# A transpose of 128 rows in place of one of 64, in a routed expert layer on one core

## The chip, the cores and the metric

The kernel runs on one core of a Trainium2 chip. The metric is device time in microseconds of one execution; times are medians of several runs. The core has five engines that run their own instruction streams in order and meet through semaphores: TensorE (PE, matmuls and transposes; its weight loads are shown apart as PEld), VectorE (DVE), ScalarE (ACT), GpSimd (POOL) and SyncE (SP, which issues most DMAs).

## What is computed

Three layers one after the other, on 2 x 576 = 1152 tokens of 512 numbers: an attention with 8 heads that keeps the 32 largest scores of a row; a dense layer with `h * cos(h)`; and a layer of eight experts, to which each token goes by its largest logit. Only the last is touched by the change:

```python
for i in range(N):
    e = expert_idx[i]
    if counts[e] < capacity:          # capacity 288
        disp[e, counts[e]] = x[i]
        pos[i] = counts[e]; counts[e] += 1; keep[i] = True
h = np.maximum(np.einsum('ecd,edf->ecf', disp, w1), 0.0)   # 512 -> 1024
y = np.einsum('ecf,efd->ecd', h, w2)                       # 1024 -> 512
for i in range(N):
    if keep[i]:
        out[i] = gate_w[i] * y[expert_idx[i], pos[i]]
```

All is in float32. Matrix products of full precision are made of two parts (`hi` rounded, `lo` the rest), as three products of a faster type.

## The kernel before

Each token's row is scattered to a DRAM buffer `xs` with `CAP` = 288 slots of `RW` = 520 numbers for each expert: 512 data, then the gate, then the token's number. The expert part works on the first `MAIN` = 192 slots of each expert; if any expert had more tokens, a conditional part (`more`, from L1055) would take the other 96, and it did not run here.

For each of the eight experts `e`:

- `gather(e)`, L949: SP brings the slots to SBUF. Slots 0 to 127 go to part 0 of `xg`, with a slot on each partition (L953). Slots 128 to 191 go to part 1, twice: to partitions 0 to 63 with all columns, and to partitions 64 to 127 with the columns from 512 on only, gate and token (L956, the loop over `a`). DVE casts the token numbers to `ti` (L958). Then come four chunks `c` of 128 columns: PE transposes part 0 (128 rows, L963) and part 1 (64 rows, L964) to a PSUM buffer `xp`, a ring of two buffers; ACT rounds the 192 columns to `xgs` (L966) and DVE subtracts to get the low part (L967). This frees the buffer.
- `expert_in(e, fc)`, L970: eight blocks, each with 4 x 2 matmuls to `hp` (L978, L980), which ACT and DVE add, clamp and split to `hc` (L983 to L991).
- `expert_out(e, a)`, L996: two output blocks `yp`, 8 units of three matmuls for slots 0 to 127 and 8 units of two for the rest (L1009), scaled with the gate by ACT (L1024, L1027) and DVE (L1029) and scattered by POOL (L1015).
- `weights2(e, i)`, L931: the float32 weights, 8 transfers of 512 KB for each expert (L936, L939), are split by ACT (`wh`, L944) and DVE (`wl`, L946), one expert or more ahead. They are kept in two sets of buffers, one for even and one for odd experts.

The order of the instructions on each engine is worked out before the program is built, by class `Plan` (L49 to L209). Each operation is declared with an engine, a cost in us, what it reads and writes, and a rank. `emit` then walks a modelled time: for each engine it takes, among the operations that could start within 0.02 us of the earliest one (L163), the one of lowest rank. It models the latency from an engine to its users (L57, `LAT`: 0.2 from PE, 0.16 from ACT, 0.14 from DVE), rings that give a buffer back after its last reader, 0.09 us for PE at a change of the kind of its output (L185), and a half clock of PE after little work (L189). Two figures of a declaration are touched: the cost of a pair of transposes, 0.4, and the number that goes with it, `duty` 0.5. The ranks put the transposes of expert `e` just ahead of the `yp` blocks of expert `e - 1`:

```python
R("rank", 90.0 + 10 * e - prm["ga"])     # L1038, ga = 4.016
gather(e)
...
R("rank", 96.0 + 10 * e + 2 * a)         # L1044
expert_out(e, a)
```

In the modelled time a gather costs SP 1.0 and the DMA 1.6 (L957).

Of the kernel before, what the change touches and what calls it, by code (L numbers as in the profile page):

```python
# [19 lines left out]
T = B * S  # L20
DM = H * D
FF = 2048
NE, F2 = 8, 1024
CAP = 288
SLOTS = NE * CAP
RW = 520
# [10 lines left out]
MAIN = 192  # L37
# [214 lines left out]
def forward(ctx, lasting, tc, kq, vn, vs_, w_in, w_out, w_gate, w1, w2, out, paired):  # L252
    nc = tc.nc
    PE, ACT, DVE, POOL, SP = nc.tensor, nc.scalar, nc.vector, nc.gpsimd, nc.sync
    prm = PRM if paired else FULL
    P = Plan(prm["tb"])
    T = P.T
# [16 lines left out]
    xs = lasting("xs", None, None)  # L274


    ident = lasting("ident", [128, 128], F32)
# [671 lines left out]
    def gather(e):  # L949
        kx = ("xg", e)  # L950

        def ld():
            SP.dma_start(T[kx][:, 0, :], xs[e * CAP:e * CAP + 128, :])  # L953
            for a in range(2):
                c = a * DM
                SP.dma_start(T[kx][64 * a:64 * a + 64, 1, c:RW], xs[e * CAP + 128:e * CAP + MAIN, c:RW])  # L956
        P.dma(1.0, 1.6, ld, r=[("xs", t) for t in range(9)], w=[kx])  # L957
        P.op("dve", 0.1, lambda: DVE.tensor_copy(T["ti", e], T[kx][:, :, DM + 1]), r=[kx], w=[("ti", e)])  # L958
        for c in range(4):
            kp, ks = ("xp", (e, c)), ("xgs", (e, c))  # L960

            def tr(c=c, kp=kp):
                PE.transpose(T[kp][:, 0:128], T[kx][:, 0, c * 128:(c + 1) * 128], ident)  # L963
                PE.transpose(T[kp][:, 128:MAIN], T[kx][0:64, 1, c * 128:(c + 1) * 128], ident[0:64, 0:64])  # L964
            P.op("pe", 0.4, tr, r=[kx], w=[kp], duty=0.5)
            P.op("act", 0.25, lambda kp=kp, ks=ks: ACT.activation(T[ks][:, 0], T[kp][:, 0:MAIN], AF.Copy), r=[kp], w=[ks])  # L966
            P.op("dve", 0.27, lambda kp=kp, ks=ks: DVE.tensor_tensor(  # L967
                out=T[ks][:, 1], in0=T[kp][:, 0:MAIN], in1=T[ks][:, 0], op=OP.subtract), r=[kp], w=[ks])
# [65 lines left out]
    for e in range(NE):  # L1034
        for i in range(8):
            R("rank", 90.0 + 10 * (e - 1) + 5 + i)
            weights2(e, i)
        R("rank", 90.0 + 10 * e - prm["ga"])  # L1038
        gather(e)
        for fc in range(8):  # L1040
            R("rank", 91.0 + 10 * e + 0.5 * fc)
            expert_in(e, fc)
        for a in range(2):
            R("rank", 96.0 + 10 * e + 2 * a)  # L1044
            expert_out(e, a)
# [90 lines left out]
```

## Time and profile before

| | |
|---|---|
| median of the runs | 705.67 us (705.2 to 707.3) |
| the profiled execution, its own time | 706.96 us |
| its span, first to last instruction | 705.1 us |
| PE busy | 596.7 us (85%) |
| DVE busy | 553.4 us (78%) |
| ACT busy | 496.0 us (70%) |
| mean granted clock of TensorE | 0.951 of full |

The expert part begins with the first gather at 523.84 us and ends with the last scatter at 698.7 us. "Busy" of PE counts overlapping records once; the end of a matmul's record is modelled, so the distance from one start to the next tells what an instruction takes of PE. The weight load of a matmul is a record of its own on PEld. A line "[0.17 <-DVE xgs L967]" behind an instruction says that its engine was idle for 0.17 us before it, and what ended that.

### The profile page before, as it was taken

Reading aid. Unit: us, or ns where it says so; the run is one execution under the profiler, and the core shown is the slowest. Engines: PE = TensorE matmul, PEld = TensorE weight load, DVE = VectorE, ACT = ScalarE, POOL = GpSimd, SP = SyncE. Lnnn points to the kernel's source line nnn. Section 1 sums busy time; section 2 is a strip of 40 time slices with the busy share of each in tenths; the row PEclk is TensorE's granted clock in tenths of the full one; section 3 lists DMA queues with packets and bytes.
Section 4 is the critical chain, followed back from the end, with each engine's and each line's share of the span. In section 5 each row is a group of like instructions: output and inputs, shape, how many; then the busy total and the mean of one; then the engine's idle time right before and its main releaser. Section 6 shows DMA issues by size and latency. Waiting matters only on the chain.

```text
span 705.1 us, 11071 instructions
## 1 busy us (share of the span) xinstructions
PE 596.7 (85%) x3611; PEld 434.8 (62%) x3611; DVE 553.4 (78%) x1654; ACT 496.0 (70%) x1004; POOL 265.2 (38%) x316
## 2 busy tenths in 40 slices
PE   3333576898999999989999899999639999999994
PEld 1122355645776655866665676666328888888893
DVE  5999999999999899999999953566115777779630
ACT  4666998999799988778877764476015777777630
POOL 3366675677345544554544432223110110011111
PEclk9999868999899999999999999999857999999998
DMA  8543552064221201100000003444023777778200
GB/s 330 198 150 122 164 163 91 1 236 172 67 89 39 76 0 38 35 1 17 1 1 1 1 17 119 140 144 150 31 78 119 230 241 223 226 257 254 71 17 16
DMA packets 29635, 76.24 MB, mean 108 GB/s; under 512 B 3966, under 2 KB 3966, under 8 KB 29568
## 3 DMA queue, kind: packets, MB, share of 16 engines
q1 hardware_dynamic: 27824, 70.68, 30.3%
q0 software_dynamic: 1744, 4.76, 1.8%
q8 instruction: 30, 0.49, 0.3%
q14 instruction: 37, 0.30, 0.2%
HBM read 63.52 MB, written 12.69 MB: 108 GB/s over the span
## 4 chain that ended last, share of the span: by engine, by line
PE 41%; DVE 34%; ACT 16%; DMA 3%; issue 3%; POOL 1%; SPq 1%; POOLq 0%; DVEq 0%; ACTq 0%
PE yp L1009 11%; DVE W L513 9%; DVE C L517 8%; PE hp L978 7%; PE x L729 7%; DVE C L509 4%; PE hp L980 3%; ACT Sp L561 2%; ACT pen L556 2%; DVE W L522 2%; DVE wt L405 2%; ACT Sp L570 2%; ACT Sp L494 2%; PE h L684 2%; DVE Sp L574 2%
## 5 line engine op out<-in xcount | busy, mean ns | idle before, releaser
L729 PE MATMUL x<-wo,hs 128*128 128x512 f32 x288 | 138.2, 603 | 0.0
L946 DVE TENSOR_TENSOR wl<-raw,wh 128x512 fp32r<-128x512 f32 x128 | 90.4, 741 | 41.9 <-ACT wh L944 38.7
L559 POOL TENSOR_TENSOR Sp<-Sp,pen 128x576 f32<-128x576 f32 x72 | 97.5, 1354 | 64.8 <-ACT pen L556 64.5
L513 DVE MAX8 W<-C 128x8 f32<-128x288 f32 x288 | 118.2, 446 | 0.6
L517 DVE MATCH_REPLACE8 C<-W,C 128x288 f32<-128x288 f32 x216 | 93.8, 440 | 0.0
L589 PE MATMUL pt<-ident,Sp 128*128 128x128 f32 x324 | 56.4, 304 | 38.6 <-ACT Sp L570 31.6
L482 PE MATMUL S<-kq 64*128 64x288 f32 x256 | 58.4, 539 | 30.8 <-ACT Sp L494 20.9
L944 ACT ACTIVATE wh<-raw 128x512 fp32r<-128x512 f32 x128 | 74.5, 622 | 9.9 <-DMA raw<-in_w_dram 6.9
L589 PEld LDWEIGHTS pt<-ident,Sp 128*128 128x128 f32 x324 | 40.4, 154 | 66.1 <-ACT Sp L570 41.0
L684 PE MATMUL h<-xh,wh 128*128 128x256 f32 x256 | 78.0, 305 | 0.5 <-ACT hs L691 0.4
L1015 POOL DMA_INDIRECT out_dram<-ot,ti x16 | 17.9, 1117 | 159.0 <-ACT ot L1024 124.8
L978 PE MATMUL hp<-xgs,wh 128*128 128x384 f32 x256 | 76.9, 370 | 0.0
L729 PEld LDWEIGHTS x<-wo,hs 128*128 128x128 f32 x288 | 49.0, 190 | 43.4 <-issue 42.7
L685 PE MATMUL h<-xl,wh 128*128 128x256 f32 x256 | 71.9, 281 | 0.0
L686 PE MATMUL h<-xh,wl 128*128 128x256 f32 x256 | 71.8, 281 | 0.0
L1009 PE MATMUL yp<-wh,hc 128*128 128x512 f32 x192 | 70.1, 405 | 0.0
L509 DVE TENSOR_TENSOR C<-Sp 128x576 f32<-128x576 f32 x72 | 64.5, 896 | 3.7 <-ACT Sp L494 2.9
L720 POOL TENSOR_TENSOR hs<-hs,ur 128x512 f32<-128x512 f32 x36 | 48.4, 1353 | 46.5 <-ACT ur L712 45.1
L980 PE MATMUL hp<-xgs,wl 128*128 128x192 f32 x256 | 65.5, 256 | 0.0
L561 ACT ACTIVATE Sp<-Sp,tb 128x576 f32<-128x576 f32 x72 | 55.7, 774 | 13.1 <-POOL Sp L559 12.9
L556 ACT ACTIVATE pen<-Sp,tb 128x576 bf16<-128x576 f32 x72 | 55.3, 768 | 6.3 <-POOL tb L549 5.5
L591 ACT ACTIVATE PT<-pt 128x384 f32<-128x384 f32 x108 | 48.5, 483 | 12.1 <-PE pt L589 12.0
(138 smaller groups left out, 1371.8 us busy)
## 6 DMA issues: line engine op xcount, KB each, us to landing
raw<-in_w_dram SPq DMA_DIRECT2D x64, 512.0 KB, 3.9
wraw<-in_w_out_dram SPq DMA_DIRECT2D x16, 512.0 KB, 3.9
wraw<-in_w_in_dram SPq DMA_DIRECT2D x16, 512.0 KB, 3.9
xs<-z SPq DMA_DIRECT2D x1, 4680.0 KB, 16.0
kq<-in_kq_dram SPq DMA_DIRECT2D x8, 576.0 KB, 7.8
v<-in_vn_dram SPq DMA_DIRECT2D x8, 320.0 KB, 5.5
v<-in_vs_dram SPq DMA_DIRECT2D x8, 320.0 KB, 3.0
out_dram<-z SPq DMA_DIRECT2D x1, 2304.0 KB, 21.0
```

The source lines that it names most:

```text
L509: DVE.tensor_tensor(out=T["C", s], in0=x[:, :, 0:HS], in1=x[:, :, HS:S], op=op)
L513: P.op("dve", 0.365, lambda r=r, i=i: DVE.max(T["W", s][:, i, LIST[r]:LIST[r] + 8], T["C", s][:, i, :]), r=[("C", s, i)], w=[("W", s, i)])
L517: P.op("dve", 0.42, lambda r=r, i=i: DVE.match_replace(T["C", s][:, i, :], T["W", s][:, i, LIST[r]:LIST[r] + 8], T["C", s][:, i, :], NEG), ...
L559: P.op("pool", 1.34, lambda i=i, kp=kp: POOL.tensor_tensor(out=T["Sp", s][:, i, :], in0=T["Sp", s][:, i, :], in1=T[kp], op=OP.subtract), r ...
L589: PE.transpose(T[kp][:, c * 128:(c + 1) * 128], P2[:, cc * 128:(cc + 1) * 128], ident)
L684: PE.matmul(o, hi, a, start=(kc == 0), stop=False, skip_group_check=True)
L729: P.op("pe", 0.86, lambda f=f, a=a: PE.matmul(T["x2", t], T[kh][:, a:a + 128], T["wo", 0][:, f, :], start=(f == 0), stop=(f == 15)), r=[kh ...
L944: P.op("act", 0.52, lambda a=a, hi=hi: ACT.activation(T[hi], T[kr][:, a * 512:(a + 1) * 512], AF.Copy), r=[kr], w=[hi])
L946: P.op("dve", 0.6, lambda a=a, hi=hi, lo=lo: DVE.tensor_tensor(out=T[lo], in0=T[kr][:, a * 512:(a + 1) * 512], in1=T[hi], op=OP.subtract), ...
L978: PE.matmul(T[kp][:, 0:2 * MAIN], T[ka][:, c:c + 128], x.rearrange("p a n -> p (a n)"), start=(kc == 0), stop=False, skip_group_check=True)
L980: PE.matmul(T[kp][:, 0:MAIN], T[kb][:, c:c + 128], x[:, 0], start=False, stop=(kc == 3), skip_group_check=True)
L1009: PE.matmul(T[kp], x, w, start=(fc + n == 0), stop=(fc == 7 and n == len(uses) - 1))
```

## The change

In `gather`, part 1 of `xg` gets the data columns of slots 128 to 255, on all 128 partitions, in one transfer of 128 rows of 512 numbers. (For the last 64 of these slots nothing of the result is used.) Gate and token columns of slots 128 to 191 come in two transfers of 64 rows of 8 numbers, to both halves of the partitions. A gather is then four DMAs, where it was three. The second transpose of a chunk reads 128 rows and writes columns 128 to 255 of `xp`; ACT and DVE still read 192 columns. The declared cost of the pair of transposes is 0.25 where it was 0.4.

```diff
         def ld():
             SP.dma_start(T[kx][:, 0, :], xs[e * CAP:e * CAP + 128, :])
+
+            SP.dma_start(T[kx][:, 1, 0:DM], xs[e * CAP + 128:e * CAP + 256, 0:DM])
             for a in range(2):
-                c = a * DM
-                SP.dma_start(T[kx][64 * a:64 * a + 64, 1, c:RW], xs[e * CAP + 128:e * CAP + MAIN, c:RW])
+                SP.dma_start(T[kx][64 * a:64 * a + 64, 1, DM:RW], xs[e * CAP + 128:e * CAP + MAIN, DM:RW])
...
                 PE.transpose(T[kp][:, 0:128], T[kx][:, 0, c * 128:(c + 1) * 128], ident)
-                PE.transpose(T[kp][:, 128:MAIN], T[kx][0:64, 1, c * 128:(c + 1) * 128], ident[0:64, 0:64])
-            P.op("pe", 0.4, tr, r=[kx], w=[kp], duty=0.5)
+                PE.transpose(T[kp][:, 128:256], T[kx][:, 1, c * 128:(c + 1) * 128], ident)
+            P.op("pe", 0.25, tr, r=[kx], w=[kp], duty=0.5)
```

## Rows read from the trace of the kernel before

**Rows 1.** Stretches: length, busy PE, PEld, DVE, ACT, POOL, granted clock, DMA share, GB/s.
```profile
596.70:605.00 8.30, 8.30 (x60) 8.30 (x59) 8.15 (x25) 7.40 (x21) 1.38 (x1) 1.00 0.96 311
605.00:617.00 12.00, 12.00 (x56) 9.17 (x55) 8.15 (x23) 8.03 (x20) 0.97 (x1) 1.00 0.59 187
```
**Rows 2.** The chain that ended last, from 560 to 700 us, shares by line.
```profile
by line: PE yp L1009 48.7%; PE hp L978 29.2%; PE hp L980 13.2%; PE xp L964 3.5%; PE xp L963 2.7%; DVE ot L1029 0.5%; ACT ot L1027 0.5%; POOL out_dram L1015 0.5%; POOLq L1053 0.4%; issue 0.1%
```
**Rows 3.** All instructions of L964: count, duration in ns (min/median/max), starts, form.
```profile
L964 PE MATMUL xp<-ident,xg x32: 271/272/367, 527.5 to 668.6; 64*128 64x64 f32 x32
```
**Rows 4.** PE in order of time, 604.5 to 609.5: start us, us, instruction.
```profile
605.57 0.27 PE L963 MATMUL xp<-ident,xg 128*128 128x128 f32 x1
605.77 0.27 PE L964 MATMUL xp<-ident,xg 64*128 64x64 f32 x1
...
606.44 0.50 PE L1009 MATMUL yp<-wh,hc 128*128 128x512 f32 x1
606.78 0.39 PE L1009 MATMUL yp<-wl,hc 128*128 128x512 f32 x1
607.01 0.40 PE L1009 MATMUL yp<-wh,hc 128*128 128x512 f32 x1
607.25 0.27 PE L963 MATMUL xp<-ident,xg 128*128 128x128 f32 x1
...
607.65 0.51 PE L1009 MATMUL yp<-wh,hc 128*128 128x512 f32 x1
608.00 0.40 PE L1009 MATMUL yp<-wl,hc 128*128 128x512 f32 x1
...
608.47 0.27 PE L963 MATMUL xp<-ident,xg 128*128 128x128 f32 x1
...
608.87 0.50 PE L1009 MATMUL yp<-wh,hc 128*128 128x512 f32 x1
```
**Rows 5.** PE in order of time, 318.3 to 319.5, attention part.
```profile
318.36 0.28 PE L686 MATMUL h<-xh,wl 128*128 128x256 f32 x1
318.47 0.82 PE L589 MATMUL pt<-ident,Sp 128*128 128x128 f32 x6
319.05 0.36 PE L684 MATMUL h<-xh,wh 128*128 128x256 f32 x1
319.25 0.28 PE L685 MATMUL h<-xl,wh 128*128 128x256 f32 x1
```
**Rows 6.** DVE in order of time, 604 to 611.
```profile
606.73 0.35 DVE L967 TENSOR_TENSOR xgs<-xp,xgs 128x192 fp32r<-128x192 f32 x1
...
607.93 0.35 DVE L967 TENSOR_TENSOR xgs<-xp,xgs 128x192 fp32r<-128x192 f32 x1
```
**Rows 7.** Weight loads in order of time, 604.5 to 609.5.
```profile
607.13 0.14 PEld L963 LDWEIGHTS xp<-ident,xg 128*128 128x128 f32 x1 [0.17 <-DVE xgs L967]
```
**Rows 8.** All engines in order of time, 517 to 534: the first two gathers.
```profile
526.04 1.09 SPq L956 DMA_DIRECT2D xg<-xs  x2
...
530.38 0.17 DVE L958 CAST ti<-xg 128x2 int32<-128x2 f32 x1 [1.64 <-DMA xg<-xs]
530.45 0.62 DVE L967 TENSOR_TENSOR xgs<-xp,xgs 128x192 fp32r<-128x192 f32 x2
...
531.56 0.69 PE L978 MATMUL hp<-xgs,wh 128*128 128x384 f32 x1
```
**Rows 9.** Stretches on both sides of the clock's rise, columns as in rows 1.
```profile
534.05:537.46 3.41, 3.41 (x14) 3.41 (x14) 1.27 (x5) 1.39 (x4) 0.00 (x0) 0.50 0.02 5
537.46:540.90 3.44, 3.44 (x26) 3.44 (x25) 2.68 (x9) 2.91 (x8) 0.00 (x0) 1.00 0.00 0
```
**Rows 10.** DMA issues by line: count, size of one, median us from issue to landing.
```profile
xg<-xs SPq DMA_DIRECT2D x8, 260.0 KB, 4.9
xg<-xs SPq DMA_DIRECT2D x8, 130.0 KB, 5.2
```
**Rows 11.** SP's DMA issues in order of time, 530 to 706: an expert's second and third.
```profile
598.78 1.10 SPq L956 DMA_DIRECT2D xg<-xs  x2
```

## The prediction

> **What bounds the kernel now.** I read the page for the span, then the busy time by stretch, then the chain of waits, then TensorE instruction by instruction. In the expert part TensorE (PE) is the bound: in the 8.30 us of an `hp` stretch and in the 12.00 us of the `yp` stretch behind it, it is busy for all of 8.30 and 12.00 us, while the vector engine (DVE) has 8.15 of each [rows 1]. The chain that ended last runs there almost only over PE, and 3.5 and 2.7 per cent of its 140 us, 8.7 us, stand on the two transposes, L964 and L963 [rows 2]. So PE time taken out of a transpose comes off the end, one for one, unless another engine is late next. DVE in the `hp` stretch (8.15 of 8.30 us) is the candidate.
>
> **The transposes.** There are 32 of the 64-row kind [rows 3], four in each of eight experts, each paired with one of 128 rows. I count by starts, since the records overlap. In the expert whose transposes begin at 605.57, L963 is followed after 0.20 us by L964, and the two first pairs end where the next `yp` matmul starts, at 606.44: 0.87 us [rows 4]. That matmul is followed by the next after 0.34 us, where 0.23 is usual (606.78 to 607.01): 0.11 more, which belongs to leaving the transposes. The third pair takes 0.40 us (607.25 to 607.65) and then 0.35 before the next one, 0.12 too many; the fourth takes 0.40 (608.47 to 608.87), and I give it the same 0.11 [rows 4]. Sum: 0.87 + 0.11 + 0.40 + 0.12 + 0.40 + 0.11 = 2.01 us for eight transposes, 0.25 each.
>
> Transposes of 128x128 alone stand in the attention part, at the same granted clock. Six in a row start at 318.47; the matmul behind them starts at 319.05 and its follower at 319.25; a matmul of that size otherwise takes 0.11 (318.36 to 318.47) [rows 5]. So six cost 319.25 - 318.47 - 0.11 = 0.67 us with their exit, 0.11 each. What differs in L964 is the tile: 64 rows and 64 columns of the array. After the change all eight of an expert are of the cheap kind: 8 x 0.11 = 0.88, which saves 1.13 us for an expert if nothing else is late.
>
> [...]
>
> **Does DVE let PE have it?** The buffer ring `xp` has two entries. The third pair needs the first entry back, which DVE frees with L967. Already now it begins with 0.17 us of waiting for it [rows 7]. L967 of the first chunk starts at 606.73 and takes 0.35; that of the second starts at 607.93 [rows 6], so the releases come at 607.08 and 608.28. DVE is full before that, so I hold these two times fixed. With cheap pairs and the order of instructions kept (two pairs, one unit of three `yp` matmuls at 0.70, a pair, a unit, a pair), PE would want the third pair at 605.57 + 0.44 + 0.70 = 606.71, and would wait to about 607.17; the fourth at 607.17 + 0.22 + 0.70 = 608.09, and would wait to 608.37, where it starts at 608.47 now. Then only 0.10 + (0.51 - 0.22) = 0.39 us of the 1.13 is left.
>
> But the order is made anew, since the planner's cost of a pair falls from 0.4 to 0.25. It takes the third pair after one unit only if its buffer comes back within 0.02 us of PE's clock. From the end of pair one, PE is free again after 0.4 + 0.09 + 0.695 = 1.19 before and 1.04 after the change (second pair, change of kind, unit). The buffer is back after 0.2 + 0.25 + 0.16 + 0.27 + 0.14 = 1.02 plus any queueing on ACT and DVE. Before, queueing of up to 0.19 was allowed; after, 0.04. In the trace pair one ends at 605.97 (605.77 + 0.20 [rows 4]) and the buffer is back at 607.08, 1.11 later: queueing 0.09, inside the old allowance. After the change pair one would end at 605.79, 0.18 earlier, with DVE as full as before: queueing 0.27, above the new one. As far as the planner's times are like the chip's, a second unit (0.70) then goes in ahead of the third pair, PE wants it at 607.41 instead of 607.17, and waits no more. I take 1.13; the bounds are 0.39 and 1.13.
>
> **By expert.** Experts 2 to 6 have the pattern shown: 5 x 1.13 = 5.65. Experts 1 and 7 have two pairs and two pairs: 2 x (0.87 + 0.11) - 0.88 = 1.08 each; in expert 7 I leave 0.2 for a wait at the third: 1.08 + 0.88 = 1.96.
>
> **The gather.** It gets a fourth DMA, the 130 KB transfer becomes one of 256 KB, and two of 2 KB remain. In the steady part it is hidden: the second transfer is issued at 598.78 [rows 11], lands after 5.2 us [rows 10] at 604.0, and its first reader starts at 605.77 [rows 4], 1.8 us later. The 260 KB transfer lands no later than the 130 KB one, 4.9 against 5.2 us [rows 10]. What SP issues behind it, weight loads, moves by one issue, about 0.5 us (1.09 for two [rows 8]); PE waits for no weights there. Without that cover each us of late landing would cost PE a us in six experts.
>
> Ahead of the first expert there is no cover. SP issues gathers 0 and 1 in a row, the last two taking 1.09 us from 526.04; DVE's `ti` cast of expert 1 waits 1.64 us for them to 530.38; behind it in DVE's queue is L967 at 530.45, which frees the buffer for expert 0's last pair, and the first `hp` matmul starts at 531.56 [rows 8]. Two more issues, one for each gather, stand ahead of the last landing, at about 0.55 each (half of 1.09), with 252 KB more to move; I take 1.0 us later. The last pair is shorter, by 0.40 - 0.22 = 0.18 at the full clock [rows 4, 5] and about 0.3 at half. So `hp` starts 0.7 us later. In the planner's times the cast (0.1) still stands ahead of L967 of the second chunk; were it behind, up to 1.64 us of waiting would go, worth half of that, 0.8, at the half clock. The clock is half (0.50) to 537.46 and full (1.00) after [rows 9], with PE busy since 531.56. If it rises at the same moment, a late start at half speed costs half: 0.35. If it rises later by as much, 0.7. If it slips by 3 us, half of the 5.9 us that PE ran before it rose, 1.5 more. I take 0.5, bounds -0.8 and 2.2.
>
> **Sum.** 5.65 + 1.96 - 0.5 = 7.1 us. The profiled execution took 706.96 us (span 705.1 and 1.9 around it), 1.3 above the median of the runs, 705.67. From its own time 699.9; against the median 698.6.
>
> **The rivals.**
> - *The order stays and PE waits for `xp`.* 5 x 0.39 + 1.96 - 0.5 = 3.4: 702.3. For it: the 0.17 us wait that is there already [rows 7]. Against it: the planner's own figures above. Chance 0.25.
> - *A worse order.* The third and fourth pair both behind one unit: the fourth then holds PE to 608.37 + 0.22 with one unit less done, 608.59 + 0.70 = 609.29 against 608.98 now, 0.31 lost for an expert: 5 x -0.31 + 1.96 - 0.5 = -0.1, so 705.8. The planner would have to see the second buffer free 0.04 us after the first; its ACT and DVE costs of 0.25 and 0.27 space them wider. Chance 0.06.
> - *Nothing saved.* The 0.20 step belongs to something other than the tile (two outputs in one buffer, say), the second transpose keeps it, and has 64 more columns to move, 0.03 us by the 0.23 for 512 columns [rows 4]: 32 x 0.03 + 0.5 = 1.5 slower, 707.2. Against it: L589 writes three outputs to one buffer and runs at 0.11 [rows 5]. Chance 0.06. [...]
> - *Slower: the gather lands late.* The DMA engines are at 0.96 in the `hp` stretch [rows 1]. If bytes set the landing, 256 KB would take 5.2 x 256 / 130 = 10.2 us, 5.0 later; 1.8 are covered, and PE stands 3.2 us in six experts: 698.6 + 19.2 = 717.8. It decides from a landing 1.8 us later; the gain is gone from 3.0. Against it: 260 KB in 4.9 us today. Chance 0.07, with smaller delays in it.
>
> **How the numbers follow.** The forecast has the other 0.56, with its own range 697.1 to 700.5 (start and expert 7 at their bounds). The range reaches to the first rival and leaves out the other three: 696.9 to 703.4. About 0.3 per cent, 2.1 us, can be told from no change here. Faster by more: forecast and first rival, 0.81; within: second and third, 0.12; slower: 0.07.
>
> **What would show it.** L964 as 128x128 with steps of 0.11 behind L963 and no long first `yp` matmul; a period of experts of 19.3 us instead of 20.4; two units ahead of the third pair, or else waits of PE or its weight load for DVE L967; the first `hp` matmul near 532.2; the gather's second transfer landing in about 5 us. Steps of 0.20 that stay, or transposes that wait for `xg`, would make the forecast wrong.

## The result, and the profile after

The changed kernel takes 698.14 us (median of 4 runs, 696.9 to 700.19) where the one before takes 706.41 (4 runs, 705.2 to 707.3): ratio 0.9887, 95% interval 0.9866 to 0.9907, 8 us less. Run again later beside other kernels it took 698.5, ratio 0.988, interval 0.9855 to 0.9905. The forecast was 698.6. It was made as 7.1 us off 705.67, the median of before in the table ahead of it; the change took 8.3 us off 706.41, so the times agree better than the savings do.

The lines of the kernel have moved by one or two: the transposes are L964 and L965 now, their users L967 (ACT) and L968 (DVE), the casts L959, the `hp` matmuls L979 and L981, the `yp` matmuls L1010.

The profiled execution has a span of 695.4 us, its own time is 697.17. The span is 9.7 us shorter than the one of before, but not all of this is the change: the first gather is issued at 521.69, 2.15 us earlier than at 523.84, behind instructions that both kernels have in the same order. In the later profile of the same changed kernel it is issued at 524.10. So I compare stretches inside the expert part, and not spans.

First TensorE in order of time, in the expert that answers to [rows 4] (start us, length us, engine, line, instruction):

```profile
599.49 0.42 PE L1010 MATMUL yp<-wh,hc 128*128 128x512 f32 x1
599.75 0.39 PE L1010 MATMUL yp<-wl,hc 128*128 128x512 f32 x1
599.98 0.39 PE L1010 MATMUL yp<-wh,hc 128*128 128x512 f32 x1
600.21 0.27 PE L964 MATMUL xp<-ident,xg 128*128 128x128 f32 x1
600.31 0.27 PE L965 MATMUL xp<-ident,xg 128*128 128x128 f32 x1
600.42 0.27 PE L964 MATMUL xp<-ident,xg 128*128 128x128 f32 x1
600.53 0.27 PE L965 MATMUL xp<-ident,xg 128*128 128x128 f32 x1
600.56 0.48 PE L1010 MATMUL yp<-wh,hc 128*128 128x512 f32 x1
600.88 0.39 PE L1010 MATMUL yp<-wl,hc 128*128 128x512 f32 x1
...
601.80 0.39 PE L1010 MATMUL yp<-wh,hc 128*128 128x512 f32 x1
602.03 0.27 PE L964 MATMUL xp<-ident,xg 128*128 128x128 f32 x1
...
602.39 0.47 PE L1010 MATMUL yp<-wh,hc 128*128 128x512 f32 x1
```

Read the starts, not the lengths: L965 is 0.27 us long as L964 of before was, but the next transpose starts 0.11 behind it and not 0.20 (the other steps between transposes were 0.20 to 0.26). Four transposes lie between 600.21 and 600.56, and the matmul behind them costs 0.32 (600.56 to 600.88) where 0.23 is usual: 0.35 + 0.09 = 0.44, for 0.87 + 0.11 before. The second visible thing is the order: two pairs, then two units of three `yp` matmuls (600.56 to 602.03), then two pairs; before it was one unit, a pair, one unit, a pair.

No instruction of PE waits for it in this expert. DVE gives the two buffers back later than PE would have wanted them after one unit (vector engine in order of time, answering to [rows 6]):

```profile
601.37 0.62 DVE L968 TENSOR_TENSOR xgs<-xp,xgs 128x192 fp32r<-128x192 f32 x2
...
604.04 0.61 DVE L968 TENSOR_TENSOR xgs<-xp,xgs 128x192 fp32r<-128x192 f32 x2
```

The first L968 starts at 601.37, 1.16 us behind the first transpose, as it did before (606.73 and 605.57 [rows 4, 6]); but the third pair comes at 602.03 only, behind the second unit. The stretches that answer to [rows 1] (length, busy time of PE, PEld, DVE, ACT, POOL, granted clock, DMA share, GB/s) show PE still without a gap, and DVE fuller in the second, 8.62 of 11.30 where it had 8.15 of 12.00 (the lengths are those of the windows asked for):

```profile
591.50:599.60 8.10, 8.10 (x59) 8.10 (x58) 7.95 (x25) 7.23 (x20) 1.11 (x1) 1.00 0.91 339
599.60:610.90 11.30, 11.30 (x58) 9.54 (x57) 8.62 (x23) 8.17 (x20) 0.97 (x1) 1.00 0.63 207
```

From the first `yp` matmul of one expert to that of the next (580.14 to 599.49 and 599.49 to 618.77 in the trace after; 584.40 to 604.86 and 604.86 to 625.32 before) it is now 19.35 and 19.28 us, where it was 20.46 and 20.46. The first such start of all and the last, after:

```profile
541.76 0.48 PE L1010 MATMUL yp<-wh,hc 128*128 128x512 f32 x1
...
676.99 0.42 PE L1010 MATMUL yp<-wh,hc 128*128 128x512 f32 x1
```

and before:

```profile
544.45 0.50 PE L1009 MATMUL yp<-wh,hc 128*128 128x512 f32 x1
...
686.68 0.42 PE L1009 MATMUL yp<-wh,hc 128*128 128x512 f32 x1
```

They are 135.23 us apart, where it was 142.24. These 7.0 us are the change's work in the steady part. The chain that ended last has 4.0 per cent of 135 us on the transposes, where it had 6.2 of 140 [rows 2]:

```profile
by line: PE yp L1010 48.0%; PE hp L979 31.2%; PE hp L981 14.1%; PE xp L964 2.1%; PE xp L965 1.9%; DVE ot L1030 0.6%; ACT ot L1028 0.5%; POOL out_dram L1016 0.5%; POOLq L1054 0.4%; issue 0.1%
```

At the start of the expert part, all engines in order of time, answering to [rows 8]:

```profile
524.83 1.09 SPq L957 DMA_DIRECT2D xg<-xs  x2
...
529.03 0.17 DVE L959 CAST ti<-xg 128x2 int32<-128x2 f32 x1 [2.55 <-DMA xg<-xs]
529.11 0.62 DVE L968 TENSOR_TENSOR xgs<-xp,xgs 128x192 fp32r<-128x192 f32 x2
...
529.85 0.67 PE L979 MATMUL hp<-xgs,wh 128*128 128x384 f32 x1
```

DVE waits 2.55 us for gather 1 in front of the cast (2.04 in the second profile), where it was 1.64. From the first gather's issue to the first `hp` matmul it is 8.16 us here (529.85 - 521.69); before, 7.72 (531.56 - 523.84). The DMA issues by line (count, KB, median us to landing), answering to [rows 10]:

```profile
xg<-xs SPq DMA_DIRECT2D x8, 260.0 KB, 2.8
xg<-xs SPq DMA_DIRECT2D x8, 256.0 KB, 5.3
xg<-xs SPq DMA_DIRECT2D x16, 2.0 KB, 4.7
```

The larger second transfer lands after 5.3 us (5.8 in the second profile of the change) where the smaller took 5.2, and after 5.2 in the run with the new gather alone, below: twice the bytes show in it here as 0.6 us at the most. (The 2.8 of the first transfer is the median of only three landings, from the first two gathers and the last; the trace has none for those between.)

### The profile page after: what moved, and what is told of

Read it like the earlier page. It is cut to its first block, busy times and chain, and to the rows that moved or that the text cites. A ratio compares the mean times of both kernels' runs of the same rounds, so it can differ in the third digit from the quotient of the medians.

```text
span 695.4 us, 11074 instructions
## 1 busy us (share of the span) xinstructions
PE 587.0 (84%) x3611; PEld 431.9 (62%) x3611; DVE 552.0 (79%) x1654; ACT 494.3 (71%) x1004; POOL 265.8 (38%) x316
## 4 chain that ended last, share of the span: by engine, by line
PE 40%; DVE 35%; ACT 15%; DMA 3%; issue 3%; POOL 1%; SPq 1%; POOLq 0%; DVEq 0%; ACTq 0%
PE yp L1010 11%; DVE W L513 9%; DVE C L517 8%; PE x L729 8%; PE hp L979 7%; DVE C L509 5%; PE hp L981 3%; ACT Sp L561 2%; DVE W L522 2%; ACT pen L556 2%; DVE wt L405 2%; ACT Sp L570 2%; ACT Sp L494 2%; PE h L684 2%; DVE Sp L574 2%
## 5 line engine op out<-in xcount | busy, mean ns | idle before, releaser
L559 POOL TENSOR_TENSOR Sp<-Sp,pen 128x576 f32<-128x576 f32 x72 | 98.9, 1373 | 63.9 <-ACT pen L556 63.3
L979 PE MATMUL hp<-xgs,wh 128*128 128x384 f32 x256 | 76.3, 368 | 0.0
L1010 PE MATMUL yp<-wh,hc 128*128 128x512 f32 x192 | 68.4, 400 | 0.0
L981 PE MATMUL hp<-xgs,wl 128*128 128x192 f32 x256 | 65.3, 255 | 0.0
```

Of the source, the lines that this page charges most:

```text
L559: P.op("pool", 1.34, lambda i=i, kp=kp: POOL.tensor_tensor(out=T["Sp", s][:, i, :], in0=T["Sp", s][:, i, :], in1=T[kp], op=OP.subtract), r ...
L979: PE.matmul(T[kp][:, 0:2 * MAIN], T[ka][:, c:c + 128], x.rearrange("p a n -> p (a n)"), start=(kc == 0), stop=False, skip_group_check=True)
L981: PE.matmul(T[kp][:, 0:MAIN], T[kb][:, c:c + 128], x[:, 0], start=False, stop=(kc == 3), skip_group_check=True)
L1010: PE.matmul(T[kp], x, w, start=(fc + n == 0), stop=(fc == 7 and n == len(uses) - 1))
```

## The experiments

Theory: a transpose on a tile of 64 rows of the array, between work on 128, makes TensorE stop on the way in and on the way out (before: a step of 0.20 us into L964 where 128 rows step at 0.11, and 0.11 more for the `yp` matmul behind the pair [rows 4, 5]); with all transposes on 128 rows these stops go, and because PE is the bound, nearly all of the time comes off, provided the order leaves DVE time to give `xp` back. Rivals: the new order alone does it; the order is without effect; the gather eats part of it.

**The new transposes in the old order.** In the changed kernel:

```diff
-            P.op("pe", 0.25, tr, r=[kx], w=[kp], duty=0.5)
+            P.op("pe", 0.4, tr, r=[kx], w=[kp], duty=0.5)
```

> The change with the declared cost of a pair left at 0.4, so that all instructions stand in the order of before (two pairs, one unit of three yp matmuls, a pair, a unit, a pair). Theory (the gain needs the new order): the pairs step at 0.11, but PE waits for DVE's L968 about 0.46 us ahead of the third pair and 0.28 ahead of the fourth in experts 2 to 6, so about 0.4 of 1.13 us is left for each: 3 to 4 us faster than before, about 703. Rival (PE work alone decides): no new waits, the whole 8 us, about 698.

Measured: 704.12 us (12 runs), ratio to before 0.9966, interval 0.9948 to 0.9983: 2.3 us of the 8. The weight loads ahead of the third and the fourth pair of the same expert (PEld in order of time):

```profile
603.88 0.14 PEld L964 LDWEIGHTS xp<-ident,xg 128*128 128x128 f32 x1 [0.71 <-DVE xgs L968]
...
605.08 0.14 PEld L964 LDWEIGHTS xp<-ident,xg 128*128 128x128 f32 x1 [0.50 <-DVE xgs L968]
```

and PE beside them:

```profile
603.21 0.40 PE L1010 MATMUL yp<-wh,hc 128*128 128x512 f32 x1
603.88 0.33 PE L964 MATMUL xp<-ident,xg 128*128 128x128 f32 x1 [0.28 <-DVE xgs L968]
```

From 603.21 to 603.88 it is 0.67 where 0.23 is usual: 0.44 us of standing, 0.46 expected; ahead of the fourth pair it is 0.46, 0.23 of standing where 0.28 was expected. The period of the experts is 20.05 to 20.25 us, 0.2 to 0.4 less than before. So the first rival of the prediction was a true picture of experts 2 to 6 in the old order, and the faster transposes alone are worth less than a third of the change. That 2.3 us came off and not the expected 3 to 4 lies in part with expert 7: around its second four transposes PE stands for 0.9 us, and the last period is 19.84 us, longer than the 19.60 of before. One of its waits (PE):

```profile
663.96 0.33 PE L964 MATMUL xp<-ident,xg 128*128 128x128 f32 x1 [0.42 <-DVE xgs L968]
```

**The new cost with the old transposes.** In the kernel before:

```diff
-            P.op("pe", 0.4, tr, r=[kx], w=[kp], duty=0.5)
+            P.op("pe", 0.25, tr, r=[kx], w=[kp], duty=0.5)
```

> The kernel before with only the declared cost of a pair set to 0.25: three DMAs, 64-row transposes, but the new order. Theory (the tile makes the steps of 0.20): a pair still costs 0.4 and its exit 0.11; fewer places where PE leaves the transposes in experts 2 to 6 (two instead of three) save about 0.05 to 0.1 us each, so 706 within 1 us. Rival (the order makes the gain): 5 us or more faster, under 702.

Measured: 705.65 us (12 runs), ratio 0.9981, interval 0.9966 to 0.9996: 0.8 us, as expected. The cost alone makes the new order: in the trace four transposes, two units and four transposes follow each other in experts 2 to 6, and each four still takes 0.97 to 0.98 us with the exit. The order alone has next to nothing to give, since PE has hardly a wait to lose. The two parts give 2.3 and 0.8, and together 8: the order is worth 5 to 6 us only once the transposes are short.

**The gather alone.** The four DMAs with the 64-row transposes and the cost of 0.4:

```diff
             SP.dma_start(T[kx][:, 0, :], xs[e * CAP:e * CAP + 128, :])
+            SP.dma_start(T[kx][:, 1, 0:DM], xs[e * CAP + 128:e * CAP + 256, 0:DM])
             for a in range(2):
-                c = a * DM
-                SP.dma_start(T[kx][64 * a:64 * a + 64, 1, c:RW], ...)
+                SP.dma_start(T[kx][64 * a:64 * a + 64, 1, DM:RW], ...)
```

> Only the four DMAs of the changed gather; the 64-row transposes and the cost 0.4 stay. Theory (the gather is hidden but for the start): the first hp matmul comes 0.8 us later against the first gather, at half clock; 0.2 to 0.8 us slower than before, 706.6 to 707.2. Rival (the larger gather holds PE in each expert): 3 us slower or more, with waits of PE for xg behind the first two experts.

Measured: 706.06 us (12 runs), ratio 0.9992, interval 0.9976 to 1.0008. Its first `hp` start lies 8.36 us behind the first gather, 0.64 later than before (0.8 expected), but the expected loss of 0.2 to 0.8 us is not found; the interval allows up to 0.6. The rival with 3 us is excluded.

**Two chunks together.** The kernel before, with its 64-row transposes, two and two:

```diff
-        for c in range(4):
+        for g in range(2):
...
+                for i, kp in enumerate(both):
+                    c = 2 * g + i
+                    PE.transpose(T[kp][:, 0:128], T[kx][:, 0, c * 128:(c + 1) * 128], ident)
+                for i, kp in enumerate(both):
+                    c = 2 * g + i
+                    PE.transpose(T[kp][:, 128:MAIN], T[kx][0:64, 1, c * 128:(c + 1) * 128], ident[0:64, 0:64])
+            P.op("pe", 0.8, tr, r=[kx], w=both, duty=0.5)
```

> The kernel before with its three DMAs, two chunks taken together (cost 0.8): two 128-row transposes, then two 64-row transposes, into two xp buffers. Read the steps from start to start at the full clock. Theory (the change of tile costs): 128 to 128 0.11, 128 to 64 0.20, 64 to 64 about 0.11 or less, and 0.20 plus 0.11 of the next matmul on the way out; four transposes 0.7 to 0.75 us with the exit where two pairs took 0.98. Rival (a 64-row transpose is slow by itself): 64 to 64 takes 0.20 too, and four take 0.8 or more. Time 704 to 708, as the buffers are now given back two at a time.

TensorE in order of time (here L965 is the 128-row transpose, L968 the one of 64 rows, L1015 the `yp` matmul; a line with x2 covers two instructions):

```profile
583.29 0.38 PE L965 MATMUL xp<-ident,xg 128*128 128x128 f32 x2
583.60 0.33 PE L968 MATMUL xp<-ident,xg 64*128 64x64 f32 x2
583.87 0.50 PE L1015 MATMUL yp<-wh,hc 128*128 128x512 f32 x1
584.20 0.39 PE L1015 MATMUL yp<-wl,hc 128*128 128x512 f32 x1
```

and the second of the two L968 alone:

```profile
583.71 0.22 PE L968 MATMUL xp<-ident,xg 64*128 64x64 f32 x1
```

The first 64-row transpose starts at 583.60, the second at 583.71: 0.11, the same as for 128 rows. The two L965 end their steps at 583.60, 0.31 behind 583.29: 0.11 and 0.20. So the 64-row transpose is not slow by itself; the change into its tile costs 0.09 on top of 0.11, and the way out 0.05 (583.71 to 583.87 is 0.16) and 0.10 of the next matmul (583.87 to 584.20 is 0.33). Out of 128-row transposes the last step and the matmul behind it make 0.12 together in the changed kernel (0.03 and 0.09); here they make 0.16 + 0.10 = 0.26. Four transposes take 0.58 + 0.10 = 0.68 us with the exit, where two pairs took 0.98. The time missed its expectation: 701.92 us (6 runs), ratio 0.9931, interval 0.9909 to 0.9954, 5 us faster than before. I had expected waits for the buffers; there is one, of 0.3 us, for a weight load. By PE's own sum, 2.01 - 2 x 0.68 = 0.65 us come off an expert, and the period of 19.75 to 19.82 us is 0.6 to 0.7 shorter than before. Of the 5 us, 4.1 lie between the first `yp` start and the last (138.16 us, before 142.24). So more than half of the gain of the change is to be had with three DMAs and 64-row transposes, by changing the tile half as often.

**One transpose more.** In the changed kernel:

```diff
                 PE.transpose(T[kp][:, 128:256], T[kx][:, 1, c * 128:(c + 1) * 128], ident)
+                PE.transpose(T[kp][:, 128:256], T[kx][:, 1, c * 128:(c + 1) * 128], ident)
```

> The change with its second transpose of each chunk done twice (32 more 128x128 transposes, same result, order of the rest unchanged). Theory (PE is the bound and such a transpose costs 0.11): 32 x 0.11 = 3.5 us slower than the change, about 701.5. Rival (there is slack on PE in the new order, DVE or the gather sets the pace): under 1 us slower, 698 to 699.

Measured: 701.12 us (6 runs), ratio to before 0.9918, interval 0.9893 to 0.9943, 2.6 us slower than the change beside it (698.5). TensorE in order of time, L966 the added transpose:

```profile
567.25 0.27 PE L965 MATMUL xp<-ident,xg 128*128 128x128 f32 x1
567.36 0.27 PE L966 MATMUL xp<-ident,xg 128*128 128x128 f32 x1
567.47 0.27 PE L964 MATMUL xp<-ident,xg 128*128 128x128 f32 x1
```

It costs 0.11 as expected, and the periods of four experts in the middle grow by 0.42 to 0.45 us, 4 x 0.11. From the first `yp` start to the last it is 137.69 us instead of 135.23 (135.39 in the second profile of the change): 2.3 to 2.5. Of the added transposes 26 lie between those starts, 2.9 us. What is missing, 0.4, is a wait that the changed kernel has and this one hasn't. In the change, the second four transposes of expert 7 stand behind their buffer (PE):

```profile
658.30 0.40 PE L1010 MATMUL yp<-wh,hc 128*128 128x512 f32 x1
658.70 0.33 PE L964 MATMUL xp<-ident,xg 128*128 128x128 f32 x1
658.87 0.27 PE L965 MATMUL xp<-ident,xg 128*128 128x128 f32 x1
```

and here they don't:

```profile
664.27 0.40 PE L1011 MATMUL yp<-wh,hc 128*128 128x512 f32 x1
664.51 0.27 PE L964 MATMUL xp<-ident,xg 128*128 128x128 f32 x1
```

From the matmul to the first transpose it is 0.40 in the change and 0.24 here, and four transposes take 0.55 there where 0.44 is usual: 0.28 us of standing in expert 7. In expert 1 the change loses 0.15 in the same way. So PE is the bound in the steady part, and a transpose is paid there in full except where PE had a wait to fill. The other six added transposes stand ahead of the first `yp` start, and what they cost can't be told from the scatter of the start.

**The change again, and with a late cast.** In the changed kernel the cast of the token numbers was put behind the last subtraction of its own expert:

```diff
-        P.op("dve", 0.1, lambda: DVE.tensor_copy(T["ti", e], T[kx][:, :, DM + 1]), r=[kx], w=[("ti", e)])
...
-            P.op("dve", 0.27, lambda kp=kp, ks=ks: DVE.tensor_tensor(
+            last = P.op("dve", 0.27, lambda kp=kp, ks=ks: DVE.tensor_tensor(
                 out=T[ks][:, 1], in0=T[kp][:, 0:MAIN], in1=T[ks][:, 0], op=OP.subtract), r=[kp], w=[ks])
+        P.op("dve", 0.1, lambda: DVE.tensor_copy(T["ti", e], T[kx][:, :, DM + 1]), r=[kx], w=[("ti", e)], after=[last])
```

> The change, with the cast of the token numbers (ti) made to come after the last xgs subtraction of its own expert, so that DVE does not stand still for gather 1 while expert 0's buffers wait behind it. Theory (the DVE stall of 2.55 us ahead of the first hp matmul is on the path): the first hp matmul comes about 2.6 us earlier against the first gather, and since TensorE then runs at half clock, 1.3 to 2.6 us come off: 695.5 to 696.8. Rival (hidden: hp waits for something else then, or gives it back where weights of expert 2 arrive): 698 as with the change.

> The change once more, beside the next one on the same chip: about 698.

> The change with the late cast once more, to be compared with the change in the same call. Theory (the stall ahead of the first hp matmul was on the path, at half clock): 1.3 to 2 us faster than the change. Rival: no difference beyond 0.5 us.

Measured: 696.85 us (5 runs), ratio to before 0.986, interval 0.9838 to 0.9882; run again 696.39 (6 runs), ratio 0.9858, interval 0.9832 to 0.9884, beside 698.5 of the change (6 runs each). The start of the expert part (all engines in order of time, first profile):

```profile
526.97 0.66 DVE L967 TENSOR_TENSOR xgs<-xp,xgs 128x192 fp32r<-128x192 f32 x2 [8.33 <-ACT xgs L966]
...
528.15 0.67 PE L979 MATMUL hp<-xgs,wh 128*128 128x384 f32 x1
...
529.18 0.16 DVE L969 CAST ti<-xg 128x2 int32<-128x2 f32 x1
```

The cast runs at 529.18 and holds nobody; the first `hp` matmul stands 5.59 us behind the first gather (522.56), 2.6 earlier than in the change; in the second pair of profiles it is 5.68 against 7.56, 1.9 earlier. 1.3 us came off (against 698.14) and 2.1 (against 698.5): the lower end of the first expectation, and just above the second's 1.3 to 2. The intervals of the two kernels overlap; both comparisons and both pairs of traces point the same way. This is the fastest version found.

## Why the prediction was right

- *The steps.* 2.01 us for an expert's transposes before and 0.88 after was read from starts in the trace of before. After, two pairs take 0.44 with their exit, twice, 0.88. The periods fell by 1.11 and 1.18 us, the one that ends at the expert shown and the one that begins there; predicted 1.13. That a tile of 64 rows is to blame was an inference from two kinds of steps; the grouped run shows it: 0.20 when the tile changes, 0.11 when it doesn't, for both tiles. What the array does in the 0.09 us between, no run shows. Each transpose has a weight load of its own, of 0.14 us for either kind before (medians 140 and 136 ns), both kinds step at 0.11, and 128 columns were no dearer than 64. One reading of the prediction was wrong: the tile is not "64 rows and 64 columns of the array". The records of L964 have 64 active rows and 128 active columns (`64*128` in [rows 3], with a weight load of 64x128); `64x64` is what is moved through. A change in the number of moved columns shows no such stop: from the last transpose, 128 columns, to the `yp` matmul, 512, the changed kernel takes 0.03 + 0.09 = 0.12 (600.53, 600.56, 600.88).
- *The order.* I worked out from the planner's costs that a second unit would come ahead of the third pair, and so that PE would not wait. That is what stands in the trace, and the run with the cost alone has the same order; whether the queueing of 0.27 us was the planner's reason, no run shows. With the old order PE waits as computed (0.44 for 0.46), and 2.3 us remain, where 3.4 had been given with experts 1 and 7 at their full gain, which they don't have there; the order alone gives 0.8. This was the step on which the sum hung most: 5 to 6 us of the 8. That the fourth pair would follow the third without a unit between I had not seen; the buffers were both back by then.
- *Expert by expert.* Experts 2 to 7 with half of expert 1 were to give 5.65 + 0.88 + 0.54 = 7.1 us between the first and the last `yp` start; the traces have 7.0 and 6.9. Within it, expert 7 waits for 0.28 us where 0.2 had been left, and expert 1 for 0.15 where nothing had.
- *The gather.* Hidden in the steady part, as forecast, but for expert 2: in the second profile of the change its second transfer lands 7.0 us after its issue, the first L965 waits for it, and PE loses 0.17 us (0.39 in the run with the old order). The weight load (PEld):

```profile
562.53 0.14 PEld L965 LDWEIGHTS xp<-ident,xg 128*128 128x128 f32 x1 [0.31 <-DMA xg<-xs]
```

  Of the start, 0.7 us late and 0.5 us lost, only the wait itself is plain: 2.55 us instead of 1.64. The first `hp` start is 8.16 us behind the first gather here, 7.56 in the second profile of the change, 7.72 before; and the gather alone costs nothing that can be found. The term of 0.5 us was within what can't be told. It may have had the wrong sign: from the first gather to the first `yp` start it is 20.08 us here and 18.41 in the second profile, where it was 20.60. The sum was 7.1 us, the steady part gave 7.0, and 8.3 came off; the rest can only lie at the start or in the scatter of the runs, and which of them isn't shown. That the forecast met the time within 0.5 us is in part luck: a saving put 1.2 us too small stood against a median of before that was 0.7 too low. How long the half clock lasts moves as much, too. Stretches after, answering to [rows 9]:

```profile
531.20:534.60 3.40, 3.40 (x15) 3.40 (x14) 0.78 (x3) 0.85 (x3) 0.00 (x0) 0.50 0.02 5
534.60:538.00 3.40, 3.40 (x25) 3.40 (x24) 2.41 (x8) 2.70 (x8) 0.00 (x0) 0.97 0.00 0
```

The granted clock rises about 4.9 us behind the first `hp` start (529.85 to some 534.7), where it had been 5.9 (531.56 to 537.46 [rows 8, 9]), and 2.6 behind it in the second profile (531.66 to 534.27). I had it rise at the same time or later.
- *The count of transposes* is as before, 32 of the second kind, with the whole tile:

```profile
L965 PE MATMUL xp<-ident,xg x32: 271/272/476, 525.1 to 659.1; 128*128 128x128 f32 x32
```

- *The next to be late.* DVE was named, and it is: in the old order in every expert, in the new one in experts 1 and 7 alone, 0.15 and 0.28 us.

## What to carry to other kernels

Here a small instruction on another tile of the array cost more than its own step of 0.11 us: 0.09 on the way in and 0.15 on the way out, in the grouped run. Read such a one from start to start over the whole group, the first matmul behind it included, and either fill it up to the tile of its neighbours (8 us here) or do several of a kind together (5 us here). Where an order is planned from costs, a shortened instruction needs its new cost as well: only 2.3 of 8 us came without it. And compare stretches that the change touches: the start of the expert part lay anywhere from 521.69 to 526.23 us over ten profiles, behind the same instructions.

## What was not expected

Two chunks together, 64-row transposes and all, gave 5 us (701.92), though the buffers come back two at a time; PE's sum told it (0.65 us for an expert), and the fear of waits was mine. The padded transposes, with no change of the tile left, still gain 0.4 to 0.5 us more for each expert: periods of 19.35 and 19.28 us against 19.75 to 19.82.
